# Fused attention and gated feed-forward: other order for the last tile's output, image sums moved between engines at the start, batch copies at other steps

One core of one Trainium2 chip. The metric is the device time of the kernel in microseconds (us), the median of several executions; lower is better. Traces give a span, from the first to the last instruction, which is 1.8 to 2.2 us shorter than the device time of the same execution.

## The reference

```python
def _attn_ref(q, kv, w_sr):            # q (4, 12288, 128), kv (4, 384, 32, 128)
    kv_pool = kv.reshape(B, H//4, 4, W//4, 4, C).mean(axis=(2, 4))
    kv_flat = kv_pool.reshape(B, -1, C) @ w_sr        # 768 keys = values per batch
    s = (q @ kv_flat.transpose(0, 2, 1)) / sqrt(C)
    a = exp(s - s.max(-1)); a /= a.sum(-1) + 1e-9
    return a @ kv_flat

def _moe_ref(x, w_gate, w_val, w_out):  # x (49152, 128), d_ff 1536
    return (maximum(x @ w_gate, 0) * (x @ w_val)) @ w_out
```

The second takes the first's result. Both sides of the product are linear in x, so the kernel leaves the softmax sum out and multiplies the final output by the squared reciprocal of that sum.

## The kernel before

There are 96 tiles of 512 tokens. A stage loop over tiles interleaves, in 12 steps per tile, the scores of one tile, the value matmuls of another, the two projections of a third and the output matmuls of a fourth. The keys of a batch come from three pairs of 128-key chunks.

```python
    def turn_add(b, pair, lines, first=False, final=False):    # sums by accumulating transposes
        n = lines.shape[2]
        for h in range(2):
            for i in range(n):
                nc.tensor.matmul(kv_Ts[b, pair][:, h], lines[:, h, i], ident, is_transpose=True,
                    start=(first and h == i == 0), stop=(final and i == n - 1), ...)
        if final:  ...  nc.vector.tensor_copy(kvT, kv_Ts[b, pair])

    def keep_sums(k, half):
        nc.vector.reciprocal(rinvs[k][:, 2 * half : 2 * half + 2], sums.pop((k, half)))
        ...
        nc.vector.tensor_tensor(inv2s[k][:, :, 0], rinv, rinv, op=ALU.mult)          # L216

    def gate_proj(k, fb):                                      # L246, L249
        nc.tensor.matmul(g_ps, wg16[...], xTs[k], start=True, stop=True)
        nc.vector.scalar_tensor_tensor(hTs[k][:, fb, :], g_ps, 0.0, vals.pop((k, fb)), ...)

    def out_proj(k, fb):                                       # L260
        for s in range(NS): nc.tensor.matmul(o_ps[:, s, :], hTs[k][:, fb, ...], wo16[:, fb, :], ...)
        if fb == NFB - 1:
            ...                                                # scaling: VectorE, or ScalarE for the last tiles
            nc.sync.dma_start(out[...], o_sb)
    ...
    # start: pair 0 by 32 transposes; for pairs 1 and 2 lines 0 and 1 are added first
    s2 = add_lines(2, (nc.gpsimd, nc.vector))                  # one half each
    # (weight loads, issued by GpSimd behind its add)
    turn_open(0, 2)
    turn_add(0, 2, s2, first=True)
    turn_add(0, 2, line(2, 2))
    turn_add(0, 2, line(2, 3), final=True)
    ...
    # inside the loop, last tile only
            if k == last and step >= 2:
                out_proj(kF, step - 2)
    for step in range(NFB - 2, NFB):
        out_proj(last - LAG, step)
```

The softmax here doesn't subtract the row's maximum and nothing guards it: scores larger than these inputs give would overflow.

## Time and profile before

| | before |
|---|---|
| device time, median (lowest to highest) | 1051.89 us (1051.74 to 1052.39) |
| span of the traced execution | 1051.3 us |
| TensorE busy | 1038.3 us, 99% |
| start: to the first value projection (L235) | 33.06 us |
| middle: from there to the last tile's first L235 | 1001.01 us |
| tail: from there to the end of the span | 17.23 us |

The three stretches of the lower half are read from the timeline of TensorE: the start times of the first L235 (33.06), and of the twelfth L235 from the end (1034.07). They add up to the span. The line of the first stands in the prediction below; that of the second is

```profile
1034.07 0.38 PE L235 MATMUL bank_ps<-xT,wv 128*128 128x512 f16 x1
```

The traced execution took 1053.17 us.

### The profile page before, as it was taken

Reading aid. Unit: us, or ns where it says so; the run is one execution under the profiler, and the core shown is the slowest. Engines: PE = TensorE matmul, PEld = TensorE weight load, DVE = VectorE, ACT = ScalarE, POOL = GpSimd, SP = SyncE. Lnnn points to the kernel's source line nnn. Section 1 sums busy time; section 2 is a strip of 40 time slices with the busy share of each in tenths; the row PEclk is TensorE's granted clock in tenths of the full one; section 3 lists DMA queues with packets and bytes.
Section 4 is the critical chain, followed back from the end, with each engine's and each line's share of the span. In section 5 each row is a group of like instructions: output and inputs, shape, how many; then the busy total and the mean of one; then the engine's idle time right before and its main releaser. Section 6 shows DMA issues by size and latency. Waiting matters only on the chain.

```text
span 1051.3 us, 26110 instructions
## 1 busy us (share of the span) xinstructions
PE 1038.3 (99%) x9996; PEld 692.5 (66%) x9996; DVE 919.5 (87%) x1771; ACT 908.6 (86%) x1746; POOL 107.3 (10%) x127
## 2 busy tenths in 40 slices
PE   8999999999999999999999999999999999999997
PEld 6666666666666666666666666666666666666665
DVE  2888889898989899988989898989898989898896
ACT  3888888888888888888888888888888888888886
POOL 2000045100000015400000003330000000000000
PEclk9999999999999999999999999999999999999999
DMA  8733256231322345523324134552331323212111
GB/s 303 124 73 83 72 185 156 51 87 31 86 56 62 71 127 150 137 62 71 67 51 86 31 86 131 158 140 47 72 80 38 86 52 66 52 46 52 46 32 46
DMA packets 125709, 90.75 MB, mean 86 GB/s; under 512 B 103312, under 2 KB 103952, under 8 KB 125584
## 3 DMA queue, kind: packets, MB, share of 16 engines
q1 hardware_dynamic: 120144, 75.85, 27.1%
q0 software_dynamic: 5440, 13.24, 7.7%
q8 instruction: 78, 1.28, 0.5%
q14 instruction: 47, 0.39, 0.1%
HBM read 52.76 MB, written 25.17 MB: 74 GB/s over the span
## 4 chain that ended last, share of the span: by engine, by line
PE 97%; DVE 1%; ACT 1%; DMA 0%; issue 0%; SPq 0%; ACTq 0%; DVEq 0%
PE bank_ps L260 24%; PE bank_ps L246 24%; PE bank_ps L235 23%; PE bank_ps L196 12%; PE bank_ps L184 12%; PE bank_ps L153 1%; PE bank_ps L165 1%; DVE hT L249 1%; DMA parts<-in_kv_dram 0%; ACT aT L185 0%; DVE o_sb L272 0%; ACT val L239 0%; ACT o_sb L270 0%; DVE kv L166 0%; DVE x L205 0%
## 5 line engine op out<-in xcount | busy, mean ns | idle before, releaser
L249 DVE SCALAR_TENSOR_TENSOR hT<-bank_ps,val 128x512 f16<-128x512 f32 x1152 | 764.7, 687 | 100.1 <-ACT val L239 71.6
L239 ACT CAST val<-bank_ps 128x512 f16<-128x512 f32 x1152 | 677.6, 589 | 118.9 <-PE bank_ps L235 115.5
L260 PEld LDWEIGHTS <-hT 128*128 128x128 f16 x4608 | 351.4, 98 | 208.6 <-issue 3.8
L260 PE MATMUL bank_ps<-wo,hT 128*128 128x128 f16 x4608 | 443.4, 219 | 2.1 <-DVE hT L249 2.0
L246 PE MATMUL bank_ps<-xT,wg 128*128 128x512 f16 x1152 | 435.7, 378 | 2.2 <-DVE hT L249 2.2
L235 PE MATMUL bank_ps<-xT,wv 128*128 128x512 f16 x1152 | 436.6, 379 | 0.0
L185 ACT ACTIVATE aT<-bank_ps 128x512 f16<-128x512 f32 x576 | 344.8, 603 | 18.8 <-PE bank_ps L184 18.8
L196 PE MATMUL bank_ps<-kv,aT 128*128 128x129 f16 x2304 | 223.5, 219 | 0.0
L196 PEld LDWEIGHTS <-aT 128*128 128x128 f16 x2304 | 177.3, 98 | 68.5 <-issue 0.4
L184 PE MATMUL bank_ps<-qT,kv 128*128 128x512 f16 x576 | 216.2, 379 | 1.5 <-DVE kv L166 1.0
L246 PEld LDWEIGHTS <-wg 128*128 128x128 f16 x1152 | 111.5, 97 | 65.4
L235 PEld LDWEIGHTS <-wv 128*128 128x128 f16 x1152 | 112.7, 98 | 0.1
L205 DVE CAST x<-bank_ps 128x256 f16<-128x256 f32 x188 | 77.9, 415 | 0.9 <-PE bank_ps L196 0.8
L77 POOL DMA_DIRECT2D q<-in_q_dram x23 | 12.5, 545 | 566.3 <-DMA qT<-q 566.1
L272 DVE TENSOR_TENSOR o_sb<-bank_ps,inv 128x512 f32<-128x512 f32 x93 | 63.3, 681 | 0.0
L136 POOL TENSOR_TENSOR s<-parts 128x512 f32<-128x512 f32 x36 | 45.3, 1269 | 166.4 <-DMA parts<-in_kv_dram 132.4
L184 PEld LDWEIGHTS <-kv 128*128 128x128 f16 x576 | 55.9, 98 | 3.4 <-DVE kv L166 2.1
L211 DVE RECIPROCAL rinv<-bank_ps 128x2 f32<-128x2 f32 x192 | 30.7, 160 | 0.7 <-ACT x L205 0.6
L216 DVE TENSOR_TENSOR inv<-rinv 128x4 f32<-128x4 f32 x96 | 20.8, 217 | 3.3
L138 POOL TENSOR_TENSOR s<-s 128x512 f32<-128x512 f32 x18 | 22.8, 1268 | 1.4
L160 DVE COPY kvT<-bank_ps 128x256 f32<-128x256 f32 x12 | 5.0, 418 | 11.7 <-PE bank_ps L153 11.7
L140 POOL TENSOR_TENSOR c<-s 128x256 f32<-128x256 f32 x18 | 13.1, 727 | 1.4
(40 smaller groups left out, 91.8 us busy)
## 6 DMA issues: line engine op xcount, KB each, us to landing
parts<-in_kv_dram SPq DMA_DIRECT2D x48, 512.0 KB, 6.2
out_dram<-o_sb SPq DMA_DIRECT2D x96, 256.0 KB, 2.2
q<-in_q_dram POOLq DMA_DIRECT2D x23, 512.0 KB, 5.1
xT<-x SPq DMA_TRANSPOSE x94, 2.5
q<-in_q_dram SPq DMA_DIRECT2D x1, 768.0 KB, 7.9
wv<-in_moe_w_val_dram POOLq DMA_DIRECT2D x2, 192.0 KB, 4.6
wg<-in_moe_w_gate_dram POOLq DMA_DIRECT2D x2, 192.0 KB, 5.0
wo<-in_moe_w_out_dram POOLq DMA_DIRECT2D x1, 384.0 KB, 9.7
```

The lines of the kernel that those rows point to most:

```text
L136: eng.tensor_tensor(s2[:, i], parts[:, 2 * i, h], parts[:, 2 * i + 1, h], op=ALU.add)
L184: nc.tensor.matmul(s_ps, kv16[:, k // NST, jc, 0:C], qT_of(k), start=True, stop=True)
L185: nc.scalar.activation(aTs[k][:, jc, :], s_ps, AF.Exp, scale=qk_scale)
L196: nc.tensor.matmul(x_ps[:, i, :], aTs[k][:, jc, s * 128 : (s + 1) * 128], kv16[:, k // NST, jc, C : 2 * C + 1], start=(jc == 0 and i == 0) ...
L205: copy(x16s[k][:, own, :], x_ps[:, :, 0:C])
L211: nc.vector.reciprocal(rinvs[k][:, 2 * half : 2 * half + 2], sums.pop((k, half)))
L235: nc.tensor.matmul(va_ps, wv16[:, fb * 128 : (fb + 1) * 128], xTs[k], start=True, stop=True)
L239: nc.scalar.copy(val, va_ps)
L246: nc.tensor.matmul(g_ps, wg16[:, fb * 128 : (fb + 1) * 128], xTs[k], start=True, stop=True)
L249: nc.vector.scalar_tensor_tensor(hTs[k][:, fb, :], g_ps, 0.0, vals.pop((k, fb)), op0=ALU.max, op1=ALU.mult)
L260: nc.tensor.matmul(o_ps[:, s, :], hTs[k][:, fb, s * 128 : (s + 1) * 128], wo16[:, fb, :], start=(fb == 0 and s == 0), stop=(fb == NFB - 1) ...
L272: nc.vector.tensor_tensor(o_sb, o_ps, inv2.to_broadcast([128, NS, 128]), op=ALU.mult)
```

## The change

Its intent: let the last tile's steps be short, and do its output afterwards by token blocks whose scaling overlaps the next block's matmuls; take 16 fp32 transposes off TensorE at the start; fill a wait there with query casts; and move the batch copies away from the steps in which x is copied.

```diff
+    def out_last(k):
+        o_banks[k] = bank([128, NS, 128])
+        for s in range(2):
+            for fb in range(NFB - 1):
+                out_add(k, fb, s, fb == 0 and s == 0)
+        for s in range(2):
+            out_add(k, NFB - 1, s, False)
+        out_scale(k, nc.vector, slice(0, 2))
+        out_store(k, slice(0, 2))
+        for s in range(2, NS):
+            for fb in range(NFB):
+                out_add(k, fb, s, False)
+            out_scale(k, (nc.scalar, nc.vector)[s % 2], slice(s, s + 1))
+        out_store(k, slice(2, NS))
 ... (start)
+    q_cast(1)
     project(0, 0)
-    for i in range(1, GRP):
-        q_cast(i)
+    q_cast(2)
+    q_cast(3)
+    q_turn_pe(1)
 ... (pair 1 alike)
-    project(0, 1)
-    for k in range(GRP - 1):
-        for jc in range(2, 4):
-            scores(k, jc)
-    s2 = add_lines(2, (nc.gpsimd, nc.vector))
+    add_lines(2, 0, nc.gpsimd, slice(0, 1))
+    s2 = add_lines(2, 0, nc.vector, slice(1, 2))
 ... (weight loads)
+    project(0, 1)
     turn_open(0, 2)
     turn_add(0, 2, s2, first=True)
-    turn_add(0, 2, line(2, 2))
-    turn_add(0, 2, line(2, 3), final=True)
+    for k in range(GRP):
+        for jc in range(2, 4):
+            scores(k, jc)
 ...
+        if k == 1:
+            for h in range(2):
+                s2 = add_lines(2, 2, nc.vector, slice(h, h + 1))
+                turn_add(0, 2, s2, final=True, chunks=[h])
 ... (loop: turn_open, project, turn_values)
-                    if step == 5:
+                    if step == 2:
-                    if step == 7:
+                    if step == 4:
-                    if step == 9:
+                    if step == 8:
-            if k == last and step >= 2:
-                out_proj(kF, step - 2)
-    for step in range(NFB - 2, NFB):
-        out_proj(last - LAG, step)
+    out_scale(last - LAG - 1, nc.scalar, slice(0, NS))
+    out_store(last - LAG - 1, slice(0, NS))
+    out_last(last - LAG)
```

More of the change, by code (lines that the diff above doesn't have):

```diff
@@ L133, in pool_pixels @@
         parts = kv_in[b, pair]
-        s2 = work.tile([128, 2, r, C], FP32, tag="kv_s2", bufs=2)
+        s2 = work.tile([128, 2, r, C], FP32, tag="kv_s2", bufs=3)
         for i in range(2):
@@ L146, in turn_open, with turn_add @@
         kv_Ts[b, pair] = bank([128, 2, 128])
-    def turn_add(b, pair, lines, first=False, final=False):
+    def turn_add(b, pair, lines, first=False, final=False, chunks=(0, 1)):
         n = lines.shape[2]
-        for h in range(2):
+        for h in chunks:
             for i in range(n):
@@ L157, in turn_add @@
                 )
-        if final:
+        if final and h == 1:
             kvT = work.tile([128, 2, 128], FP32, tag="kvT", bufs=2)
@@ L177 @@
     aTs, x_banks, x16s, xTs, rinvs, inv2s, sums = {}, {}, {}, {}, {}, {}, {}
-    hTs, o_banks, vals = {}, {}, {}
+    hTs, o_banks, o_sbs, vals = {}, {}, {}, {}
     def scores(k, jc):
@@ L253, in gate_proj, with out_add @@
             xTs.pop(k)
+    def out_add(k, fb, s, first):
+        nc.tensor.matmul(
+            o_banks[k][:, s, :], hTs[k][:, fb, s * 128 : (s + 1) * 128], wo16[:, fb, :],
+            start=first, stop=(fb == NFB - 1), skip_group_check=True,
+        )
     def out_proj(k, fb):
@@ L257, in out_proj @@
             o_banks[k] = bank([128, NS, 128])
-        o_ps = o_banks[k]
         for s in range(NS):
-            nc.tensor.matmul(
-                o_ps[:, s, :], hTs[k][:, fb, s * 128 : (s + 1) * 128], wo16[:, fb, :],
-                start=(fb == 0 and s == 0), stop=(fb == NFB - 1), skip_group_check=True,
-            )
-        if fb == NFB - 1:
-            hTs.pop(k)
-            o_sb = work.tile([128, NS, 128], FP32, tag="o_sb", bufs=3)
-            o_ps, inv2 = o_banks.pop(k), inv2s.pop(k)
-            if k + LAG + 1 > NT:
-                for s in range(NS):
-                    nc.scalar.mul(o_sb[:, s, :], o_ps[:, s, :], inv2[:, s])
-            else:
-                nc.vector.tensor_tensor(
-                    o_sb, o_ps, inv2.to_broadcast([128, NS, 128]), op=ALU.mult
-                )
-            nc.sync.dma_start(
-                out[k // GRP * GRP * T : (k // GRP + 1) * GRP * T, :].rearrange(
-                    "(p i s) c -> i p s c", p=128, i=GRP
-                )[k % GRP], o_sb,
-            )
+            out_add(k, fb, s, fb == 0 and s == 0)
@@ new lines, in out_scale @@
+    def out_scale(k, engine, own):
+        if k not in o_sbs:
+            o_sbs[k] = work.tile([128, NS, 128], FP32, tag="o_sb", bufs=3, name="o_sb")
+        if engine is nc.scalar:
+            for s in range(own.start, own.stop):
+                nc.scalar.mul(o_sbs[k][:, s, :], o_banks[k][:, s, :], inv2s[k][:, s])
+        else:
+            nc.vector.tensor_tensor(
+                o_sbs[k][:, own, :], o_banks[k][:, own, :],
+                inv2s[k][:, own].to_broadcast([128, own.stop - own.start, 128]), op=ALU.mult,
+            )
@@ new lines, in out_store @@
+    def out_store(k, own):
+        nc.sync.dma_start(
+            out[k // GRP * GRP * T : (k // GRP + 1) * GRP * T, :].rearrange(
+                "(p i s) c -> i p s c", p=128, i=GRP
+            )[k % GRP][:, own], o_sbs[k][:, own],
+        )
+        if own.stop == NS:
+            for tiles in (hTs, o_banks, inv2s, o_sbs):
+                del tiles[k]
+    def out_last(k):
+        o_banks[k] = bank([128, NS, 128])
+        for s in range(2):
+            for fb in range(NFB - 1):
+                out_add(k, fb, s, fb == 0 and s == 0)
+        for s in range(2):
[7 more added lines that the diff above has]
+        out_store(k, slice(2, NS))
@@ L316, in line, with add_lines @@
         return kv_in[0, pair][:, dh]
-    def add_lines(pair, engines):
-        s2 = work.tile([128, 2, r, C], FP32, tag="kv_s2", bufs=2)
-        for h in range(2):
-            engines[h].tensor_tensor(
-                s2[:, h], line(pair, 0)[:, h], line(pair, 1)[:, h], op=ALU.add
-            )
+    def add_lines(pair, dh, engine, chunks=slice(0, 2)):
+        if (pair, dh) not in s2s:
+            s2s[pair, dh] = work.tile([128, 2, r, C], FP32, tag="kv_s2", bufs=3, name="kv_s2")
+        s2 = s2s[pair, dh]
+        engine.tensor_tensor(
+            s2[:, chunks], line(pair, dh)[:, chunks], line(pair, dh + 1)[:, chunks], op=ALU.add
+        )
         return s2
+    s2s = {}
     q_cast(0)
@@ L336 @@
     turn_values(0, 0)
-    for i in range(1, GRP):
+    for i in range(2, GRP):
         q_turn_pe(i)
@@ L341 @@
             scores(k, jc)
-    s2 = add_lines(1, (nc.vector, nc.vector))
     turn_open(0, 1)
-    turn_add(0, 1, s2, first=True)
+    turn_add(0, 1, add_lines(1, 0, nc.vector), first=True)
     attend(0, 0)
-    turn_add(0, 1, line(1, 2))
-    turn_add(0, 1, line(1, 3), final=True)
+    for h in range(2):
+        s2 = add_lines(1, 2, nc.vector, slice(h, h + 1))
+        turn_add(0, 1, s2, final=True, chunks=[h])
     attend(1, 0)
-    project(0, 1)
-    for k in range(GRP - 1):
-        for jc in range(2, 4):
-            scores(k, jc)
-        if k == 0:
-            turn_values(0, 1)
-    s2 = add_lines(2, (nc.gpsimd, nc.vector))
+    add_lines(2, 0, nc.gpsimd, slice(0, 1))
+    s2 = add_lines(2, 0, nc.vector, slice(1, 2))
     for own in (slice(0, D_FF // 2), slice(D_FF // 2, D_FF)):
@@ L364 @@
     q_load(2)
+    project(0, 1)
     turn_open(0, 2)
     turn_add(0, 2, s2, first=True)
-    turn_add(0, 2, line(2, 2))
-    turn_add(0, 2, line(2, 3), final=True)
-    for jc in range(2, 4):
-        scores(GRP - 1, jc)
+    for k in range(GRP):
+        for jc in range(2, 4):
+            scores(k, jc)
+        if k == 0:
+            turn_values(0, 1)
+        if k == 1:
+            for h in range(2):
+                s2 = add_lines(2, 2, nc.vector, slice(h, h + 1))
+                turn_add(0, 2, s2, final=True, chunks=[h])
+        if k == 2:
+            project(0, 2)
     attend(0, 1)
-    project(0, 2)
     attend(1, 1)
@@ L410 @@
                 out_proj(kO, step)
+                if step == NFB - 1 and k < last:
+                    out_scale(kO, nc.vector if kF < NT - 2 else nc.scalar, slice(0, NS))
+                    out_store(kO, slice(0, NS))
             if kF < NT:
```

## The prediction

> **What bounds the kernel now.** I read the page first: how long each engine is busy, then the chain that ended last.
>
> ```profile
> PE 1038.3 (99%) x9996; PEld 692.5 (66%) x9996; DVE 919.5 (87%) x1771; ACT 908.6 (86%) x1746; POOL 107.3 (10%) x127
> ...
> PE 97%; DVE 1%; ACT 1%; DMA 0%; issue 0%; SPq 0%; ACTq 0%; DVEq 0%
> ```
>
> TensorE is busy for 1038.3 of 1051.3 us and holds 97% of the path. So the middle can only become shorter by dropping TensorE work, and the change drops none there. What else is left is some 13 us in which TensorE is idle, plus the store after it. The waits by window put most of it at the two ends; in the long middle it is small:
>
> ```profile
> PE bank_ps L246 <- DVE hT L249: 2.2, 6, 0.5
> ```
>
> That is 2.2 us in six waits between 100 and 1000 us. Columns: total us, times, longest.
>
> The start is the timeline of TensorE from 5 us on (start, length, line, count, idle before):
>
> ```profile
> 6.63 5.63 PE L153 MATMUL bank_ps<-ident,parts 128*128 128x128 f32 x32 [0.19 <-DMA parts<-in_kv_dram]
> 12.77 0.70 PE L165 MATMUL bank_ps<-kvT,w_sr_f 128*128 128x256 f32 x2 [0.52 <-DVE kvT L160]
> 13.99 0.61 PE L184 MATMUL bank_ps<-qT,kv 128*128 128x512 f16 x2 [0.52 <-DVE kv L166]
> ...
> 18.33 1.92 PE L153 MATMUL bank_ps<-ident,parts 128*128 128x128 f32 x16
> ...
> 22.05 0.60 PE L184 MATMUL bank_ps<-qT,kv 128*128 128x512 f16 x2 [0.52 <-DVE kv L166]
> ...
> 25.09 1.91 PE L153 MATMUL bank_ps<-ident,parts 128*128 128x128 f32 x16
> ...
> 28.89 0.61 PE L184 MATMUL bank_ps<-qT,kv 128*128 128x512 f16 x2
> ...
> 33.06 0.38 PE L235 MATMUL bank_ps<-xT,wv 128*128 128x512 f16 x1
> ```
>
> Each of the three pairs of image chunks must be summed, turned, projected and scored in series; scores of the pairs start at 13.99, 22.05 and 28.89, and the full-rate stage at 33.06. The first turn (32 in 5.6 us) is paced by loads. The loads set later steps too:
>
> ```profile
> 20.16 1.27 POOL L321 TENSOR_TENSOR s<-parts 128x512 f32<-128x512 f32 x1 [18.38 <-DMA parts<-in_kv_dram]
> ```
>
> So the second line of pair 2 lands at 20.16. The windows of 1 us show about 415 GB/s until 21.6, and a line is 0.52 MB, so lines land some 1.25 us apart: estimate, the last line of pair 1 at 17.6 and the last of all at 21.9.
>
> The end, from the same view of all engines:
>
> ```profile
> 1036.66 0.62 PE L260 MATMUL bank_ps<-wo,hT 128*128 128x128 f16 x8 [0.69 <-DVE hT L249]
> ...
> 1044.35 1.14 ACT L270 ACTIVATE o_sb<-bank_ps,inv 128x128 f32<-128x128 f32 x4
> ...
> 1045.36 0.60 ACT L239 CAST val<-bank_ps 128x512 f16<-128x512 f32 x1
> 1046.00 0.69 DVE L249 SCALAR_TENSOR_TENSOR hT<-bank_ps,val 128x512 f16<-128x512 f32 x1 [1.00 <-ACT val L239]
> ...
> 1046.75 0.40 PE L260 MATMUL bank_ps<-wo,hT 128*128 128x128 f16 x4 [1.30 <-DVE hT L249]
> 1047.18 1.14 ACT L270 ACTIVATE o_sb<-bank_ps,inv 128x128 f32<-128x128 f32 x4 [1.22 <-PE bank_ps L260]
> ```
>
> ScalarE puts the four scalings of tile 94 ahead of the last value cast, so the last product, the last four output matmuls, the last scalings and the last store all stand in series. The scalings end at 1048.32 and the span at 1051.3: the store costs 2.98 us.
>
> **What the Trainium skill says.** "VectorE: DVE Perf Modes", the section on the TRN2 errata, gives (N+151)/0.96 ns for an fp32 tensor_tensor: 691 ns at N=512; the trace has 681 to 684 for the adds of L321, so I take 0.65 us each in a row and 1.3 us for the new 128x1024 add. "SBUF — State Buffer", section Who interferes with whom: a VectorE instruction with two SBUF inputs and a GpSimd instruction that reads SBUF exclude each other for the whole instruction. The trace agrees: the tiny squaring of L216 has 161/162/1175 ns as min/median/max, and the executions of 1.07 us at 177.85 and 1.18 us at 646.48 lie beside GpSimd adds that began at 177.63 and 646.36. "TensorE: Matmul & The Clock Gate", section Back-to-back issue gap: 134 cycles for 128 columns, 56 ns; the trace has 0.22 us for four (55 ns), and double that for fp32 (16 turns in 1.77 us on the chain, 111 ns). "DMA: Bandwidth & Descriptors", Anatomy of one DMA: a fixed 2.0 us and bytes at 436 GB/s (fitted on another issue path); the trace's 256 KB store lands in 2.0 us, of which about 0.65 is data, so a half store saves an estimated 0.3 us and not half.
>
> **Part 1: less image summing on TensorE.** For pairs 1 and 2 the lines 2 and 3 are added on VectorE before turning: 16 turns fewer (2 x 8) x 111 ns = 1.78 us of TensorE, against two adds of 0.65 us per pair on a VectorE that is mostly idle there. It isn't a saving of 1.78, since waits take part of it. Step by step:
> - Query casts between key copies. Before, three casts stood between the key copy (ends 13.94) and the next query copies, so the scores of tile 1 began at 15.52. Now the cast of tile 1 fills the wait for L165, and its scores begin at about 15.1. But VectorE then has the whole first add of pair 1 (1.3 us from about 15.85, one instruction), so its turns start at about 17.2, against 16.98 before: nothing gained yet.
> - Adds of lines 2 and 3 of pair 1 wait for the landing, 17.6; done at 18.25 and 18.9. Last turn ends 19.4, keys' copy about 20.1, projection from 20.1 (before 20.86): 0.75 gained.
> - In VectorE's new order the half add of pair 2 stands BEFORE the copy of pair 1's keys, and it waits for the landing at 20.16, where GpSimd's half begins too. By the exclusion both end at 22.1 (0.65 + 1.27 from 20.16). TensorE in its new order turns these eight before the scores of pair 1. So the scores start at about 22.6 (23.0 if VectorE goes first): 0.5 us LATER than 22.05, with 0.9 us of turning already done.
> - Then: four scores and the turn of values to 23.75; VectorE copies the values to 24.05 and adds lines 2 and 3 to 25.35; last turn 25.85; scores of tile 2; projection 26.35; scores of tile 3; keys ready 27.3; 16 value matmuls to 27.7; pair 2's scores at about 27.7, against 28.89. ScalarE sets the next 4 us (eight exponentials at 0.507) and comes free at 28.3 against 29.32.
> Gain at the start: 1.0 us (0.4 to 1.6).
>
> **Part 2: batch copies moved in the step.** The turn, projection and turn of values go from steps 5, 7, 9 to 2, 4, 8. Their number stays. A tile with them takes 11.28 us and one without 10.51 (the scalings at 732.20, 743.48 and 753.99); the difference of 0.77 is what TensorE's own six extra instructions need (0.22 + 0.43 + 0.11), so there is no wait to win. What moves is GpSimd's third pair, which waited 1.9 us for the turn at 182.95 and now is released some 2.6 us earlier; this may shift which L216 is hit. The 2.2 us of L246 waits stem from those hits at steps that aren't moved: I give this part 0, with 0.7 either way.
>
> **Part 3: the last tile.** Before, from step 2 on each step of the last tile held eight output matmuls and lasted 0.88 us (L235 at 1038.00, 1038.88). Now only tile 94's four stay: 0.655 us. Step 0 begins at 1033.85 and has its L235 at 1034.07, so step 11 has it at 1041.27. VectorE runs products at 0.60 us from tile 95's first at 1035.9, so the last begins at 1042.5 and ends at 1043.2. TensorE meanwhile does 22 output matmuls for two token blocks (1.2 us from 1041.7, waiting a little for product 10), then two with the last product to 1043.36; 12 for block 2 to 1044.02; 12 for block 3 to 1044.68. Results take 0.25 us to come out; a VectorE scaling of 128 elements is an estimated 0.26 (120+128 cycles by the same errata table, which gives 0.39 for 256 where the trace has 0.415): o_sb complete at 1045.2, store 2.7, end 1047.9. That is 3.4 less than 1051.3; I count 3.2 for bank waits that I can't see. Tile 94's scalings (1.14 us) follow the last cast at 1042.3 and end before block 2 needs ScalarE, at 1044.25; its whole store is out before the last.
>
> **Sum:** 1051.9 - 1.0 - 0 - 3.2 = 1047.7 us.
>
> **Rivals.** (a) The start gives nothing, or loses: VectorE's queue holds pair 1's keys behind an add that waits for a load, and the scores slip past 23.5. For it: the order, the 20.16 landing and the exclusion. Against: the gain then comes at pair 2, whose turns are half as many. Then about 1048.7. (b) The start gives all of TensorE's 1.78 us: loads land earlier than I think and exclusion doesn't bite; 1046.9. (c) The last tile becomes bound by VectorE or by banks: seven free banks hold about 3.5 steps, and products lag their matmuls by some 2.3 us, which is just 3.5 steps of 0.655. If each step went to 0.70, the end is 0.5 later: 1048.2. (d) The moved copies collide with the copies of x in step 5 or with GpSimd: nine tiles by 0.3 us, 2.7 lost, 1050.4; TensorE's 0.77 of cover speaks against.
>
> **Range and chances.** Ends are nearly independent: start 0.4 to 1.6, end 2.6 to 3.6, middle within 0.7. Combined: 1046.4 to 1049.3. Two per cent is 21 us, far more than all idle time: faster 0.01, same 0.98, slower 0.01.
>
> **What would show it.** Right: first L235 near 32.0 (before 33.06); pair 1's scores a little later than 22.05, pair 2's near 27.7; the half add of pair 2 on VectorE or GpSimd stretched; steps of the last tile at 0.655 us, no wait of 0.69 us for the first product of the last tile, 13.9 us from the last tile's first L235 to the end of the span (before 1034.07 to 1051.3, 17.2), and a last store of about 2.7. TensorE busy about 1.8 us less. Wrong: first L235 outside 31.4 to 32.7, L246 waits over 3 us in the middle, or last-tile steps over 0.7 us.

## The result, and the profile after

The changed kernel took 1050.51 us (1049.98 to 1050.84, 4 runs) against 1051.93 in the same rounds. Ratios here are the mean time of one kernel's fast runs over that of the other's of the same rounds, so not quite the ratio of the medians quoted. It is 0.9985, 95% interval 0.9968 to 1.0003. The predicted gain was three times the measured one, 4.2 us against 1.4, and the time lies outside the range. The interval contains 1, so that there is a gain at all was settled only later, by experiment 9.

The page's first and fourth parts, of the changed kernel:

```profile
PE 1035.6 (99%) x9980; PEld 688.8 (66%) x9980; DVE 920.5 (88%) x1776; ACT 909.5 (87%) x1743; POOL 107.8 (10%) x127
...
PE 96%; DMA 2%; DVE 1%; issue 0%; SPq 0%; POOL 0%; ACT 0%; DVEq 0%; POOLq 0%
```

Line numbers shift: L256 is the output matmul (L260 before), L272 and L274 are the scalings, L345 the line adds (L321 before). TensorE is busy 2.7 us less, and its share of the path is the same but for some loading at the start. The traced spans are 1051.3 and 1048.8. They differ by 2.5 us and not by 1.4, since the traced execution of the kernel before was a long one. By stretch:

| | predicted change | before | after | traced change |
|---|---|---|---|---|
| start | -1.0 | 33.06 | 32.81 | -0.25 |
| middle | 0 | 1001.01 | 1000.21 | -0.80 |
| tail | -3.2 | 17.23 | 15.78 | -1.45 |

**Tail.** The timeline of all engines of the changed kernel (start, length, engine, line, count, idle before and its releaser):

```profile
1033.02 0.38 PE L235 MATMUL bank_ps<-xT,wv 128*128 128x512 f16 x1
...
1041.12 1.15 ACT L272 ACTIVATE o_sb<-bank_ps,inv 128x128 f32<-128x128 f32 x4
...
1041.59 0.95 PE L256 MATMUL bank_ps<-wo,hT 128*128 128x128 f16 x14 [0.21 <-DVE hT L249]
1042.58 0.42 DVE L274 TENSOR_TENSOR o_sb<-bank_ps,inv 128x256 f32<-128x256 f32 x1 [0.45 <-PE bank_ps L256]
1043.06 0.83 PE L256 MATMUL bank_ps<-wo,hT 128*128 128x128 f16 x12 [0.52 <-DVE o_sb L274]
...
1043.93 0.37 ACT L272 ACTIVATE o_sb<-bank_ps,inv 128x128 f32<-128x128 f32 x1 [1.66 <-PE bank_ps L256]
1044.35 0.83 PE L256 MATMUL bank_ps<-wo,hT 128*128 128x128 f16 x12 [0.46 <-ACT o_sb L272]
...
1045.28 0.29 DVE L274 TENSOR_TENSOR o_sb<-bank_ps,inv 128x128 f32<-128x128 f32 x1 [2.28 <-PE bank_ps L256]
```

TensorE waits for each scaling before it goes on (0.52 and 0.46 us): scaling and matmuls alternate instead of overlapping. The output is complete at 1045.57, 12.55 us after the last tile's first L235 (1033.02), where the prediction had 11.13. And the store takes 3.23 us from there to the end, where it had 2.7.

**Start.** The timelines of TensorE, of GpSimd and of VectorE, changed kernel:

```profile
20.50 0.67 PE L165 MATMUL bank_ps<-kvT,w_sr_f 128*128 128x256 f32 x2 [0.16 <-DVE kvT L160]
22.32 1.10 PE L153 MATMUL bank_ps<-ident,kv_s 128*128 128x128 f32 x8 [1.14 <-POOL kv_s L345]
23.25 0.59 PE L184 MATMUL bank_ps<-qT,kv 128*128 128x512 f16 x2
...
28.65 0.59 PE L184 MATMUL bank_ps<-qT,kv 128*128 128x512 f16 x2
...
32.81 0.38 PE L235 MATMUL bank_ps<-xT,wv 128*128 128x512 f16 x1
```

```profile
20.50 1.76 POOL L345 TENSOR_TENSOR kv_s<-parts 128x512 f32<-128x512 f32 x1 [18.72 <-DMA parts<-in_kv_dram]
```

```profile
20.45 0.69 DVE L345 TENSOR_TENSOR kv_s<-parts 128x512 f32<-128x512 f32 x1
21.21 0.42 DVE L166 TENSOR_SCALAR kv<-bank_ps 128x256 f16<-128x256 f32 x1
```

VectorE's half of the add began 0.05 us before GpSimd's; GpSimd's, 1.27 us long in the kernel before, took 1.76 here. TensorE stood 1.14 us before the turns of pair 2, and the scores of pair 1 behind them began at 23.25, 1.2 us later than before.

**Middle.** The waits between 100 and 1000 us of the changed kernel (total, times, longest), against 2.2 us in six before:

```profile
PE bank_ps L246 <- DVE hT L249: 1.7, 4, 0.5
```

One of these waits in the kernel before, from the timelines of GpSimd, VectorE and TensorE:

```profile
177.63 1.27 POOL L136 TENSOR_TENSOR s<-parts 128x512 f32<-128x512 f32 x1 [1.87 <-DMA parts<-in_kv_dram]
```

```profile
177.85 1.07 DVE L216 TENSOR_TENSOR inv<-rinv 128x4 f32<-128x4 f32 x1
```

```profile
179.57 0.38 PE L246 MATMUL bank_ps<-xT,wg 128*128 128x512 f16 x1 [0.39 <-DVE hT L249]
```

and the same place in the changed kernel, where the load landed 1.1 us later:

```profile
177.67 0.16 DVE L216 TENSOR_TENSOR inv<-rinv 128x4 f32<-128x4 f32 x1
```

```profile
178.75 1.27 POOL L136 TENSOR_TENSOR s<-parts 128x512 f32<-128x512 f32 x1 [2.09 <-DMA parts<-in_kv_dram]
```

The squaring of four numbers takes 0.16 us, or 1.07 when a GpSimd add has just begun. VectorE is then late with the products that free the gate banks, and TensorE waits 0.39 us. In the changed trace GpSimd came after it. So the 0.8 us could be a matter of when loads land, not of the change. The experiments had to tell.

### The profile page after: what moved, and what is told of

The parts are those of the page before. It is cut to its first block, busy times and chain, and to the rows that moved or that the text cites. A ratio compares the mean times of both kernels' runs of the same rounds, so it can differ in the third digit from the quotient of the medians.

```text
span 1048.8 us, 26047 instructions
## 1 busy us (share of the span) xinstructions
PE 1035.6 (99%) x9980; PEld 688.8 (66%) x9980; DVE 920.5 (88%) x1776; ACT 909.5 (87%) x1743; POOL 107.8 (10%) x127
## 3 DMA queue, kind: packets, MB, share of 16 engines
q8 instruction: 78, 1.28, 0.5%
## 4 chain that ended last, share of the span: by engine, by line
PE 96%; DMA 2%; DVE 1%; issue 0%; SPq 0%; POOL 0%; ACT 0%; DVEq 0%; POOLq 0%
PE bank_ps L256 24%; PE bank_ps L246 24%; PE bank_ps L235 24%; PE bank_ps L196 12%; PE bank_ps L184 11%; DMA parts<-in_kv_dram 2%; DVE hT L249 1%; PE bank_ps L165 0%; PE bank_ps L153 0%; POOL kv_s L345 0%; SPq L127 0%; ACT aT L185 0%; PE bank_ps L173 0%; DVE x L205 0%; DVE o_sb L274 0%
## 5 line engine op out<-in xcount | busy, mean ns | idle before, releaser
L256 PEld LDWEIGHTS <-hT 128*128 128x128 f16 x4608 | 351.4, 98 | 203.6 <-issue 4.0
L256 PE MATMUL bank_ps<-wo,hT 128*128 128x128 f16 x4608 | 443.5, 219 | 1.2 <-DVE o_sb L274 0.5
L246 PE MATMUL bank_ps<-xT,wg 128*128 128x512 f16 x1152 | 435.7, 378 | 1.7 <-DVE hT L249 1.7
L235 PE MATMUL bank_ps<-xT,wv 128*128 128x512 f16 x1152 | 436.6, 379 | 0.0
L246 PEld LDWEIGHTS <-wg 128*128 128x128 f16 x1152 | 111.4, 97 | 65.4
L235 PEld LDWEIGHTS <-wv 128*128 128x128 f16 x1152 | 112.7, 98 | 0.1
L274 DVE TENSOR_TENSOR o_sb<-bank_ps,inv 128x512 f32<-128x512 f32 (+1 forms) x95 | 64.0, 673 | 2.7 <-PE bank_ps L256 2.7
```

What stands on the lines that cost most here:

```text
L235: nc.tensor.matmul(va_ps, wv16[:, fb * 128 : (fb + 1) * 128], xTs[k], start=True, stop=True)
L246: nc.tensor.matmul(g_ps, wg16[:, fb * 128 : (fb + 1) * 128], xTs[k], start=True, stop=True)
L256: nc.tensor.matmul(o_banks[k][:, s, :], hTs[k][:, fb, s * 128 : (s + 1) * 128], wo16[:, fb, :], start=first, stop=(fb == NFB - 1), skip_gr ...
L274: nc.vector.tensor_tensor(o_sbs[k][:, own, :], o_banks[k][:, own, :], inv2s[k][:, own].to_broadcast([128, own.stop - own.start, 128]), op= ...
```

## The experiments

Twelve runs were made, of eleven new kernels and of the changed one again, with 5 executions each; every one gave the right result. "Against" gives the median of the kernel before in the same rounds. The first L235 is, as above, the first value projection; middle and tail are the stretches of the table.

**1. tail_only**: the kernel before with `out_last` and what belongs to it, start and steps as before.

> The kernel before with the last tile's new order alone. My theory: this part gives most of the gain, but less than the 3.2 us I predicted, since TensorE waits for the readers of the output bank: first L235 of the last tile to the end of the span takes about 15.8 us as in the changed kernel (before 17.2), so time 1.4 us below before, and the first L235 stays near 33.0. Rival: the tail's gain in the changed kernel depended on the shifted start and steps, then it is under 0.7 us here.

Measured: 1049.97 us against 1052.37, ratio 0.9983 (0.9970 to 0.9997). Tail 15.77 us, as in the changed kernel; first L235 at 32.19; middle 999.44 with three waits of L246. The tail's 1.45 us are thus this part's own. The first L235 came 0.87 us earlier than in the trace of before although its start is the same code: the first sign that starts differ by that much between executions.

**2. start_only**: the kernel before with the new start (and three buffers for the line sums).

> The kernel before with the new start alone (casts between key copies, fewer turns). My theory: the saved turns are eaten by the turns of pair 2 standing ahead of the scores of pair 1 and by the exclusion of VectorE's and GpSimd's adds (GpSimd's add stretched to about 1.7 us): first L235 0 to 0.5 us earlier than 33.06, time within 0.5 us of before. Rival (the prediction): 1.0 us faster, first L235 at 32.0.

Measured: 1052.25 against 1052.37, ratio 0.9998 (0.9985 to 1.0010). First L235 at 32.81, GpSimd's add 1.76 us. The new start alone gains nothing that can be seen. Its trace fell on an execution with seven L246 waits of 3.2 us together and a middle of 1002.24.

**3. steps_only**:

```diff
-                    if step == 5:      # turn_open, turn_add
+                    if step == 2:
-                    if step == 7:      # project
+                    if step == 4:
-                    if step == 9:      # turn_values
+                    if step == 8:
```

> The kernel before with the batch copies at steps 2, 4, 8 alone. Theory A: it costs and gains nothing by itself; the middle changes only by the number of waits of L246 for VectorE (six in the kernel before, four after), some 0.4 us each, which depend on when loads land: time within 0.5 us of before, and the middle (first L235 to first L235 of the last tile, 1001.0 us before, 1000.2 after) shorter only as far as such waits are fewer. Theory B: the moved copies themselves free TensorE: middle at 1000.2 with six waits still there.

Measured: 1051.97 against 1052.37, ratio 0.9997 (0.9984 to 1.0009). Middle 1000.19 with four waits of 1.4 us. Of A's two halves, the first holds (no visible gain). Middle and waits went down together, so B, which wanted six waits to stay, fails as it was put.

**4. tail_banks**: the changed kernel with a bank for each part of the last output that is scaled by itself.

```diff
         for s in range(2, NS):
+            o_banks[k] = bank([128, NS, 128])
             for fb in range(NFB):
-                out_add(k, fb, s, False)
+                out_add(k, fb, s, fb == 0)
```

> The changed kernel with a PSUM bank of its own for each part of the last output that is scaled alone (tokens 0 and 1, 2, 3). My theory: TensorE waited 0.52 and 0.46 us for the scalings only since they read the bank that it writes next; these two waits vanish, the last matmul comes 1.0 us earlier, time 1.0 us below the changed kernel, tail 14.8 us. Rival: TensorE would wait for something else there (products, weight loads), and the tail stays at 15.8 us.

Measured: 1049.29 against 1052.37, ratio 0.9970 (0.9957 to 0.9982). The tail is 14.44 us, 0.4 shorter than expected. The timeline of all engines:

```profile
1041.43 2.30 PE L256 MATMUL bank_ps<-wo,hT 128*128 128x128 f16 x38 [0.21 <-DVE hT L249]
...
1042.42 0.42 DVE L274 TENSOR_TENSOR o_sb<-bank_ps,inv 128x256 f32<-128x256 f32 x1 [0.45 <-PE bank_ps L256]
1043.10 0.37 ACT L272 ACTIVATE o_sb<-bank_ps,inv 128x128 f32<-128x128 f32 x1 [0.98 <-PE bank_ps L256]
1043.77 0.29 DVE L274 TENSOR_TENSOR o_sb<-bank_ps,inv 128x128 f32<-128x128 f32 x1 [0.92 <-PE bank_ps L256]
```

The 38 last matmuls run through in 2.30 us. The output is complete 11.20 us after the last tile's first L235, against 12.55: 1.35 us gained, 0.98 of it the two waits, the rest presumably the emptied pipeline after each. This is within 0.1 us of the 11.13 that the prediction worked out without bank waits. The Trainium skill, "PSUM — Partial Sum Buffer", section PSUM bank collisions raise a hardware error, says that two engines may not touch one bank on the same partitions at once, even in different columns, and that the program has to keep them apart. That is presumably why the built program has these waits; no run here shows a collision itself. What the runs show is that the waits go when each part has a bank of its own. In the changed kernel one call of `bank` holds all four token blocks, so the scaling of one block and the matmuls of the next always met in it.

**5. start_keys**: tail_banks with the keys of pair 1 ahead of the adds of pair 2.

```diff
+    project(0, 1)
     add_lines(2, 0, nc.gpsimd, slice(0, 1))
     s2 = add_lines(2, 0, nc.vector, slice(1, 2))
 ...
-    project(0, 1)
-    turn_open(0, 2)
-    turn_add(0, 2, s2, first=True)
 ...
         if k == 0:
             turn_values(0, 1)
+            turn_open(0, 2)
+            turn_add(0, 2, s2, first=True)
```

> tail_banks, with the keys of pair 1 projected and copied before VectorE's half add of pair 2, and the first turns of pair 2 behind the first scores of pair 1. In five runs with the new start the first L235 came 12.3 us after GpSimd's add of pair 2 could begin. My theory: order alone costs the predicted 1.0 us (the keys wait in VectorE's queue behind an add that waits for a load, the scores on TensorE behind turns that wait for GpSimd): scores of pair 1 at about 21.6 instead of 23.25, first L235 at 31.5 and 11.0 us after the landing, tail unchanged at 14.4, time 1.3 us below tail_banks. Rival: pair 2's landing sets the start whatever the order; first L235 again 12.3 us after it.

Measured: 1048.22 against 1052.02, ratio 0.9966 (0.9953 to 0.9978). The timelines of TensorE, then of VectorE:

```profile
22.12 0.60 PE L184 MATMUL bank_ps<-qT,kv 128*128 128x512 f16 x2 [0.52 <-DVE kv L166]
...
32.34 0.38 PE L235 MATMUL bank_ps<-xT,wv 128*128 128x512 f16 x1
```

```profile
23.73 1.29 DVE L346 TENSOR_TENSOR kv_s<-parts 128x512 f32<-128x512 f32 x2 [0.56 <-DMA parts<-in_kv_dram]
```

GpSimd's add began at 20.92 and took 1.26 us again, so the first L235 came 11.42 us after its start, against 12.3 in the other new starts: 0.9 us gained by order alone in this trace (0.6 and 0.7 in all_best and keys_direct below, which have the same order: 11.67 and 11.58). The timed ratio can't confirm it: it is only 0.0004 below that of tail_banks. It is less than the 1.3 expected, and the VectorE line says why: now the last lines of pair 2 are waited for, until 23.73. The first L235 follows 8.61 us later, as it does after 24.20 in the changed kernel. I had put that landing at 21.9.

**6. no_excl**: tail_banks with both halves on VectorE; GpSimd only copies one value of the line.

```diff
-    add_lines(2, 0, nc.gpsimd, slice(0, 1))
-    s2 = add_lines(2, 0, nc.vector, slice(1, 2))
+    nc.gpsimd.tensor_copy(touch, line(2, 1)[:, 1, 0, 0:1])
+    for h in range(2):
+        s2 = add_lines(2, 0, nc.vector, slice(h, h + 1))
```

> tail_banks, with both halves of pair 2's first add on VectorE; GpSimd only touches one value of the line, so that its weight loads still wait for the same landing. My theory: the exclusion of the two engines' adds is worth 0.5 us and GpSimd's slowness another 0.4: no add is stretched, pair 2's turns end about 1 us sooner, scores of pair 1 at 22.3 instead of 23.25 where the landing is at 20.5, first L235 11.4 us after the landing instead of 12.3. Rival: it is only the order (then 12.3 stays).

Measured: 1048.23 against 1052.02, ratio 0.9968 (0.9956 to 0.9981). The scores of pair 1 began at 22.64, 0.6 us earlier than in the changed kernel, but the first L235 at 33.15, 12.39 us after the landing: nothing gained there. The timeline of VectorE:

```profile
24.53 1.29 DVE L346 TENSOR_TENSOR kv_s<-parts 128x512 f32<-128x512 f32 x2 [0.85 <-DMA parts<-in_kv_dram]
```

The last lines were waited for until 24.53. The weight loads began at 20.89 here, against 22.13 in start_keys, so they may have slowed the last image lines. But by the semaphores in the traces the last line landed 3.8 us after the second line of its pair here, 2.8 in start_keys and 3.7 in tail_banks, whose weight loads began at 22.66 only. So why it came late is open. The expectation failed: the exclusion's cost is real (1.76 us against 1.26), but another load took its place as the bound.

**7. sq_act**: tail_banks with the squaring on ScalarE, at step 2 of the next tile. The reciprocals (`rinv`) live longer for it and get six buffers instead of three.

```diff
-        inv2s[k] = work.tile([128, NS, 1], FP32, tag="inv2", bufs=8, name="inv2")
-        nc.vector.tensor_tensor(inv2s[k][:, :, 0], rinv, rinv, op=ALU.mult)
+        unsquared.append((k, rinv))
+    def square_sums():
+        while unsquared:
+            k, rinv = unsquared.pop(0)
+            inv2s[k] = work.tile([128, NS, 1], FP32, tag="inv2", bufs=8, name="inv2")
+            nc.scalar.activation(inv2s[k][:, :, 0], rinv, AF.Square)
 ... (loop)
+            if step == 2:
+                square_sums()
```

> tail_banks, with the squaring of the reciprocal sums (VectorE, two SBUF inputs) moved to ScalarE at step 2 of the next tile. In six traces the middle from the first L235 to the last tile's was 998.4 to 999.0 us plus the waits of L246 for VectorE. Theory: these waits come from the squaring shut out by GpSimd's adds, so no wait of L246 is left, the middle is 998.7 us in this run, and the runs spread less (under 0.6 us) at 0.8 us below tail_banks. Rival: the waits have another cause (DVE full when copies of a batch are due) and stay at 2 to 7, or ScalarE's added work (96 x some 0.2 us) costs as much.

Measured: 1047.29 (1046.80 to 1047.74) against 1052.02, ratio 0.9955 (0.9941 to 0.9969). No wait of L246 is left, the middle is 997.88 us, 0.8 less than the 998.7 I expected, and the gain over tail_banks is 1.6 us by the two ratios, twice what I expected (their intervals overlap; the traced middles differ by 1.73). The runs spread by 0.94 us, against 1.28 in tail_banks: narrower, but not under 0.6. ScalarE's new work, from the page's groups (busy us, mean ns, idle before):

```profile
L221 ACT ACTIVATE inv<-rinv 128x4 f32<-128x4 f32 x96 | 19.8, 208 | 0.0
```

These 19.8 us, of which ScalarE's busy total shows 7.3 more than in tail_banks (916.8 against 909.5), cost no time that can be seen. ScalarE was busy for 87% before.

**8. one_store**: tail_banks with one store at the end.

```diff
         out_scale(k, nc.vector, slice(0, 2))
-        out_store(k, slice(0, 2))
 ...
-        out_store(k, slice(2, NS))
+        out_store(k, slice(0, NS))
```

> tail_banks, with one store of the last tile's 256 KB at the end instead of two of 128 KB. I predicted that half a store saves 0.3 us; the traces show 3.21 to 3.24 us from the last scaling to the end with half a store and 2.90 to 2.98 with a whole one. Theory: splitting the store costs 0.3 us rather than saving any, so 2.95 here, tail 14.15. Rival: the 3.2 has to do with the earlier end of the kernel or the order of scalings, and a whole store then takes 3.5.

Measured: 1048.56 against 1052.02, ratio 0.9970 (0.9957 to 0.9982). From the last scaling to the end 2.99 us; tail 14.17, against 14.44 in tail_banks. All whole stores took 2.90 to 2.99 us there, all half stores 3.19 to 3.30. Splitting the store costs 0.3 us in the traces; the timed ratio equals that of tail_banks, so timing alone doesn't resolve it.

**9. after_again**: the changed kernel unaltered.

> The changed kernel unaltered, timed again, since its first interval reached from 0.9968 to 1.0003. Theory: 1.4 us below before from the tail alone, ratio about 0.9986, with a spread of 1 us from the number of L246 waits. Rival: 4 us below, as predicted.

Measured: 1050.51 (1049.25 to 1051.98) against 1052.96, ratio 0.9980 (0.9967 to 0.9992). Four L246 waits, middle 1000.14, tail 15.73, first L235 at 32.53. The change is faster by about 2 us, half of what I predicted.

**10. before_sq**: the kernel before with sq_act's edit alone.

> The kernel before with the squaring on ScalarE alone. Theory: the middle of the kernel before (1001.0 us in its trace) is long by the squarings shut out by GpSimd, whatever the steps of the batch copies: middle 998 us here as in sq_act (997.9), no wait of L246, time 2 us below before and spread under 1 us. Rival: sq_act owed its short middle to the moved batch copies, then the middle here stays near 1000.

Measured: 1049.59 (1049.45 to 1050.37) against 1052.96, ratio 0.9973 (0.9959 to 0.9987). Middle 997.88 us, no wait of L246, with the batch copies at their old steps. Tile by tile, the traces of before and before_sq differ in six places of the middle only, by 0.32 to 0.66 us each and 3.12 us together: those are the six waits of L246. All other tiles agree within 0.025 us. The squaring alone sets the middle's excess; where the copies stand makes no difference once it is gone.

**11. all_best**: start_keys, one_store and sq_act together.

> start_keys, one_store and sq_act together, on the output banks of tail_banks. Theory: the three act on different stretches, so the gains add: middle 997.9, tail 14.15, first L235 at 32.3, span about 1044.4, time 1046.3. Rival: a shorter start only moves the first tiles' waits (loads of the weights and of the second group of queries), the middle gets longer by as much, and the time stays at sq_act's 1047.3.

Measured: 1046.38 (1046.00 to 1046.67) against 1052.96, ratio 0.9939 (0.9926 to 0.9951). First L235 at 32.20, middle 997.88, tail 14.12. Stretch by stretch the gains add. This beats both kernels.

**12. keys_direct**: all_best with the last two lines of pair 2 turned without an add.

```diff
-            for h in range(2):
-                s2 = add_lines(2, 2, nc.vector, slice(h, h + 1))
-                turn_add(0, 2, s2, final=True, chunks=[h])
+            turn_add(0, 2, line(2, 2))
+            turn_add(0, 2, line(2, 3), final=True)
```

> all_best, but with the last two lines of pair 2 turned by TensorE without an add, as in the kernel before. In the three new starts I opened the first L235 came 8.6 us after VectorE's adds of those lines began, which in start_keys began when the load landed (23.7). Theory: once the landing sets the start, adding first only lengthens the way from landing to keys (two adds of 0.65 us and four turns, against eight turns of 0.9 us on a TensorE that idles there), so turning directly is 0.5 to 1.0 us faster although TensorE does eight more turns. Rival: TensorE's work counts (eight turns, 0.9 us) and this is slower than all_best.

Measured: 1046.23 (1046.02 to 1046.50), ratio 0.9938 (0.9925 to 0.9950): the same as all_best. Both sides of the expectation failed. The timeline of TensorE, of all_best and then of keys_direct:

```profile
24.34 1.26 PE L153 MATMUL bank_ps<-ident,kv_s 128*128 128x128 f32 x8 [0.61 <-DVE kv_s L351]
```

```profile
23.84 1.91 PE L153 MATMUL bank_ps<-ident,parts 128*128 128x128 f32 x16
```

Eight turns after two adds end at 25.60, sixteen without any at 25.75; counted from the start of GpSimd's add (20.53 and 20.78) that is 5.07 and 4.97. The eight turns saved cost as much time in waiting as they save in work.

## Why the prediction was wrong, point by point

**Tail: 1.45 us instead of 3.2. Settled.** The steps of the last tile did take 0.655 us, TensorE no longer waited 0.69 us for the first product, and the last value cast no longer stood behind scalings. So rival (c) is out. Two terms failed. The first is "then two with the last product to 1043.36; 12 for block 2 to 1044.02; 12 for block 3 to 1044.68": it let TensorE write the bank that the scalings read. tail_banks shows 1.35 us for that, and without it the sum I worked out holds within 0.1 us. I had set aside 0.2 us "for bank waits that I can't see", though the edit shows all four blocks in one bank. The second is "so a half store saves an estimated 0.3 us": one_store shows that it costs 0.3. Together with the reserve: 1.35 + 0.5 - 0.2 makes 1.65 of the 1.75 missing.

**Start: nothing instead of 1.0 us. The cause is shown.** Six traces have the new start unaltered (changed kernel 32.81, start_only 32.81, after_again 32.53, tail_banks 33.25, sq_act 32.84, one_store 33.06: mean 32.88), and four the old one (before 33.06, tail_only 32.19, steps_only 32.75, before_sq 32.48: mean 32.62). By the prediction's own sign, a first L235 outside 31.4 to 32.7, the start was wrong, and rival (a), "The start gives nothing, or loses", is what came, by the queue order and the exclusion that it names (the scores slipped to 23.25, not past 23.5).

Most of the scatter goes when the times are counted from the start of GpSimd's add of pair 2, which marks the landing of its load. The first L235 then follows 12.30 to 12.31 us later in all six new starts, and 12.22 to 12.23 us later in three of the four old ones. In the trace of before, from which I predicted, it is 12.90. On this count I forecast 11.84 (32.0 - 20.16), 1.06 us less. Of these, 0.68 were that one trace's lateness, and 0.46 were costs that I understated; the new start really loses 0.1 us.

The lateness hid behind a misreading of mine: I took the first turns to be "paced by loads". In the trace of before they run on as one block of 32, the first 18 in 3.87 us (0.21 us each), the rest at 0.11, and end at 12.26. In steps_only, whose start is the same code, each line is turned as it lands:

```profile
8.34 1.09 PE L153 MATMUL bank_ps<-ident,parts 128*128 128x128 f32 x8 [0.54 <-DMA parts<-in_kv_dram]
9.59 1.09 PE L153 MATMUL bank_ps<-ident,parts 128*128 128x128 f32 x8 [0.16 <-DMA parts<-in_kv_dram]
10.85 1.09 PE L153 MATMUL bank_ps<-ident,parts 128*128 128x128 f32 x8 [0.17 <-DMA parts<-in_kv_dram]
```

Why TensorE was slow there is open (the profile's granted clock is 1.00 in both).

The mechanism that I named in part 1 was right and is seen: the key copy behind a half add in VectorE's queue, the turns ahead of the scores, the exclusion. Its cost was understated in two terms. "So the scores start at about 22.6 (23.0 if VectorE goes first)": VectorE did go first, and the landing was at 20.50 in the trace, so it was 23.25. And "pair 2's scores at about 27.7" became 28.65. start_keys gets back 0.9 us by order alone, and then meets the landing of the last lines at 23.7, which I had estimated at 21.9.

**Middle: 0 predicted, 0.8 us traced, just outside the 0.7 allowed.** "The 2.2 us of L246 waits stem from those hits at steps that aren't moved" holds: before_sq removes the waits with the steps unmoved. Rival (d), moved copies that cost 2.7 us, is out by steps_only. This table is over all traces:

| kernel | L246 waits, us (times) | middle, us |
|---|---|---|
| tail_banks | 0.8 (2) | 999.61 |
| no_excl | 1.0 (2) | 999.57 |
| tail_only | 1.0 (3) | 999.44 |
| steps_only | 1.4 (4) | 1000.19 |
| start_keys | 1.4 (4) | 1000.10 |
| one_store | 1.5 (3) | 1000.27 |
| after_again | 1.6 (4) | 1000.14 |
| after | 1.7 (4) | 1000.21 |
| before | 2.2 (6) | 1001.01 |
| start_only | 3.2 (7) | 1002.24 |
| sq_act, before_sq, all_best, keys_direct | 0 (0) | 997.88 in each |

The middle differs by 2.8 us among kernels with the squaring on VectorE, and by nothing among the four without it. The squaring's own length explains it. In these ten traces 55 squarings are stretched beyond 0.25 us; each overlaps an add of GpSimd and ends 0.02 us after it. TensorE waits after every one longer than 0.75 us and after no other, and each wait ends 0.65 us after the squaring's end (43 waits, with four under 0.15 us that the list leaves out). So the rival that VectorE is merely full when a batch's copies are due is out.

The waits listed are not the whole loss. Tile by tile against before_sq, each hit of the kernel before costs the squaring's length less 0.52 us, while the wait listed is its length less 0.68. Summed over the squarings longer than 0.52 us, that gives the middle's excess over 997.88 within 0.13 us in all ten traces (before: 3.11 of 3.13), so nothing of it is left over.

One thing stays open: whether the new steps lower the number of hits. steps_only alone is at 0.9997 with an interval that contains both 0 and 1 us, and the middle's mean is 1000.90 us in the three traces with the old steps, 1000.01 in the seven with the new ones, with 2.8 us between equal steps. The 0.8 us by which this pair of traces was better in the middle can't be credited to the change.

**Range.** I allowed each stretch 0.5 to 0.7 us about its worked-out value. Executions with the same start already scatter by 0.9 us there (32.19 to 33.06) and, as the table shows, by up to 2.8 us in the middle. The chances by two per cent were right, since all idle time together is far below that.

## What to carry to other kernels

When a tail is split so that one engine empties a result while TensorE makes the next, look whether both lie in one PSUM bank; here nothing overlapped until each part had a bank of its own. Where two engines shut each other out, look in the trace for tiny instructions with a long maximum: here 0.16 us of work, moved to an engine with room, was worth 2.8 us (before_sq). And before a gain of a microsecond is forecast or put down to a part, split several traces into the same stretches: equal code differed by up to that much, and the one trace that I predicted from was late by 0.7 us at the start.

## What the Trainium skill lacked or had wrong

- "SBUF — State Buffer", section Who interferes with whom: the exclusion is stated, and that the later of the two blocks fully; the runs agree (GpSimd's add 1.76 us beside VectorE's add, 1.26 to 1.27 without; the squaring 1.07 instead of 0.16). What it lacks is the price further on: a squaring held for 0.75 us or more made TensorE wait by up to 0.60 us, and moving 96 squarings shortened the middle from 999.4 to 1002.2 us to 997.88.
- "PSUM — Partial Sum Buffer", section PSUM bank collisions raise a hardware error: the rule is stated; its price is not. Two alternations in one bank cost 1.35 us, of which 0.98 are listed as waits.
- "DMA: Bandwidth & Descriptors", section Anatomy of one DMA: from its fixed 2.0 us and 436 GB/s I estimated 0.3 us less for half a store. On this issue path the half store landed in 1.9 us instead of 2.0, but the end of the kernel came 3.19 to 3.30 us after the last scaling, against 2.90 to 2.99 with a whole one.
- No page gives a way to work out when a load that shares the DMA engines with others lands: I estimated 21.9 us for the last image line from the byte rate, and VectorE waited for it until 23.6 to 24.5 us in three runs.
